# A tuned attention-plus-MLP kernel: order of the first loads and a new order of steps

## The chip, the core and the metric

The kernel runs on one core of one Trainium2 chip. TensorE (PE) multiplies, VectorE (DVE), ScalarE (ACT) and GpSimd (POOL) work elementwise, and the queue of SyncE (SP) issues nearly all DMAs. The metric is the device time of the program in microseconds; lower is better. All times below are microseconds unless marked otherwise.

## The reference

The input x is [2048, 512] in bf16. It is layer-normalised, goes through two branches, and both results are added to x:

```python
xn = _layernorm(x, axis=-1)
return x + _A_ref(xn, A_wqkv, A_w_phi, A_wo) + _B_ref(xn, B_w1, B_b1, B_w2)
```

Branch A is linear attention with 32 heads of 16. Queries and keys are multiplied per head by w_phi [16, 16]; the feature map is softmax(p) beside softmax(-p):

```python
phi_k = jnp.concatenate([_softmax(pk, axis=-1), _softmax(-pk, axis=-1)], axis=-1)
kv = jnp.einsum("bhsf,bhsd->bhfd", phi_k, v)
num = jnp.einsum("bhqf,bhfd->bhqd", phi_q, kv)
```

The numerator is divided by phi_q times the sum of phi_k, and the heads are multiplied by wo [512, 512]. Branch B is h = xn w1 + b1 with 1792 columns, h tanh(softplus(h)), and w2 back to 512.

## The kernel before

The 2048 rows are 16 tiles of 128, in four groups of four. x, all weights, the transposed normalised rows xnT and the activations acts of branch B stay on chip. w_phi is folded into the weights: the keys' and the queries' parts of wqkv are turned, multiplied by Wbd (w_phi laid out as a block diagonal) and copied back, so that a projection of xn gives the logits of the feature map directly.

The order of all work is written out by hand in the string STEPS (line 24). Each step is a name and its arguments; a number behind @ is the PSUM bank (there are six, plus one double bank called kv) and a letter a or v says whether ScalarE or VectorE makes the copy. Lines 620 to 643 map names to functions and run the steps. Each engine executes its instructions in the order in which the steps issue them, and a wait blocks what stands behind it on that engine. A step that takes a bank waits until the copy out of its last content is done.

The names that matter here:

- LS i, RS i, AZ i (lines 547 to 557): mean and variance of tile i of the first group on VectorE, its 1/sqrt on POOL (two instructions), its centring on VectorE. TP i turns the centred tile by TensorE, TC i copies it into xnT.
- TW kt and TK kt (566 to 578): TensorE turns the natural half (kt 0 and 1) of the keys' weights wkp, ScalarE copies it into wT. The other half of wT comes turned by a DMA (line 482). WB makes Wbd from w_phi (wsrc). F0 kt (line 146) folds, FD kt copies the fold back into wkp. LP (line 196) makes the first two key logits, eight matmuls; with "i" the two tiles alternate, so each FD releases one pair.
- PB and CB turn the bias b1 and copy it. KM makes a mask from constants.
- LN g, AP g k, DX g: statistics, centring plus DMA transposes, and loads of the later groups. WT, F, FC: the queries' weights, turned by DMA and folded later. DW loads w2 and wo.
- V t and VC t: value projection and its copy. L s i and LC s i: logits of tile i in stage s (0 to 3 keys, 4 to 7 queries) and their copy; WL the same in the kv bank. H u and M u: one of 56 blocks of the hidden layer and its activation.
- E s p, X s k, S s k: extremes and subtraction (five VectorE instructions), exponential on ScalarE, sums on VectorE. R and N: reciprocal and normalisation of the keys. A g k: accumulation of kv. KV masks it. W s k: weights of the queries and their DMA transposes. Q, G, C: the queries' product, its copies, the division with a DMA transpose.
- O t, P t, Y t: second layer, output projection, residual and store. OH, PH, YH do the last tile in two parts.

Ahead of the steps stand the first loads (lines 476 to 492) and WARM + SHORT dummy matmuls of 512 and 128 columns on constants (line 517). The loads of x, wqkv and w1 go through SP's queue, those of the bias and of w_phi through ScalarE's. The order on SP is x tile 0, x tile 1, the natural half of the keys' weights, the turned half, then the rest.

Of the kernel before, what the change touches and what calls it, by code (L numbers as in the profile page):

```python
# [21 lines left out]
STEPS = """
TW 0 @0; TW 1 @1; LS 0; LS 1; RS 0; PB @2; KM; AZ 0; TK 0 a; RS 1; DX 2; WB; TP 0 @3; F0 0 @4; AZ 1;
TP 1 @5; TK 1 a; FD 0 a; TC 0 v; F0 1 @0; F0 2 @1; FD 1 a; F0 3 @3; FD 2 a; TC 1 v; LS 2; RS 2; FD 3
a; LS 3; CB; LP i @4,5; V 1 @0; AZ 2; LC 0 0 v; RS 3; AZ 3; TP 2 @1; V 0 @3; LC 0 1 v; TC 2 a; TP 3
@2; L 0 2 @4; VC 0 a; TC 3 v; H 0 @1; L 0 3 @5; LC 0 2 a; LC 0 3 a; LN 1; H 1 @3; H 2 @2; H 3 @4; M
0; M 1; H 4 @5; VC 1 a; M 2; H 5 @1; H 6 @3; H 7 @0; M 3; M 4; H 8 @2; M 5; M 6; H 9 @4; H 10 @5; E
0 0; M 7; H 11 @1; AP 1 0; L 1 0 @3; WL 1; AP 1 1; M 8; V 6 @0; E 0 1; X 0 0; LN 2; VC 6 v; X 0 1;  # L30
DX 3; LN 3; LC 1 0 a; L 1 3 @2; LC 1 3 a; AP 2 0; AP 2 1; WL 2; M 9; H 12 @0; H 13 @3; M 10; H 14
@2; H 15 @4; H 16 @5; M 11; M 12; M 13; M 14; M 15; M 16; H 17 @1; LC 1 1 a; S 0 1; H 18 @0; M 17;
AP 3 0; AP 3 1; M 18; S 0 0; H 19 @3; H 20 @2; H 21 @4; H 22 @5; M 19; M 20; H 23 @1; H 24 @0; M 21;
M 22; M 23; M 24; LC 1 2 v; E 1 0; E 1 1; H 25 @3; H 26 @2; H 27 @4; H 28 @5; H 29 @1; V 2 @0; VC 2
v; DW 3; M 25; M 26; M 27; M 28; M 29; R 0 0 a; L 2 1 @3; L 2 0 @2; WT; L 2 2 @4; LC 2 0 a; R 0 1 a;
LC 2 1 v; F 0 @5; F 1 @1; N 0 0; FC 0 a; FC 1 a; F 2 @0; V 3 @3; LC 2 2 a; X 1 1; L 3 0 @2; VC 3 a;
FC 2 v; N 0 1; F 3 @5; FC 3 a; LC 3 0 v; L 2 3 @0; X 1 0; V 4 @1; L 3 3 @4; DW 2; LC 2 3 v; L 3 1
@2; VC 4 a; LC 3 3 a; V 8 @0; V 5 @3; VC 5 a; V 9 @5; A 0 0; VC 9 a; LC 3 1 a; E 2 0; E 2 1; L 4 0
@1; S 1 0; L 3 2 @4; VC 8 a; S 1 1; X 2 0; H 30 @3; S 2 0; LC 4 0 a; L 4 3 @5; LC 4 3 a; LC 3 2 a; L
4 2 @2; LC 4 2 a; L 4 1 @0; V 7 @1; VC 7 v; A 0 1; R 1 0 a; LC 4 1 a; E 3 0; R 1 1 a; H 31 @5; H 32  # L40
@4; H 33 @2; E 3 1; H 34 @0; H 35 @1; M 30; M 31; N 1 0; M 32; M 33; M 34; H 36 @3; M 35; H 37 @5; H
38 @4; M 36; M 37; M 38; H 39 @2; N 1 1; M 39; H 40 @0; H 41 @1; H 42 @3; M 40; M 41; H 43 @5; A 1
0; A 1 1; M 42; V 13 @4; L 6 1 @2; E 4 0; E 4 1; V 10 @0; V 15 @1; VC 10 v; M 43; L 6 0 @3; O 0 @5;
X 3 0; V 12 @0; X 2 1; X 3 1; LC 6 0 v; LC 6 1 v; X 4 0; S 3 0; VC 13 a; R 3 0 a; VC 15 a; S 2 1; R
2 1 a; V 11 @3; O 1 @2; VC 11 a; L 5 0 @4; VC 12 a; L 6 3 @1; R 2 0 a; LC 6 3 a; S 4 0; LC 5 0 a; L
6 2 @3; LC 6 2 a; S 3 1; L 5 1 @0; LC 5 1 a; L 5 2 @1; L 5 3 @4; R 3 1 a; LC 5 2 a; LC 5 3 a; V 14
@3; VC 14 a; H 44 @0; N 2 0; N 3 0; N 3 1; H 45 @1; X 4 1; M 44; N 2 1; H 46 @4; H 47 @3; M 45; M
46; A 2 0; W 4 0 v; M 47; A 2 1; A 3 0; S 4 1; A 3 1; H 48 @0; M 48; H 49 @1; M 49; H 50 @4; L 7 0
@3; H 51 @0; M 50; M 51; H 52 @1; H 53 @4; KV; W 4 1 v; E 5 0; E 5 1; M 52; M 53; H 54 @0; M 54; Q 0
0; G 0 0; E 6 0; H 55 @1; O 2 @4; M 55; X 5 0; Q 0 1; LC 7 0 a; S 5 0; O 3 @0; G 0 1; Q 1 0; L 7 3  # L50
@1; C 0 a; G 1 0; LC 7 3 a; L 7 1 @3; LC 7 1 a; W 5 0 v; Q 1 1; G 1 1; X 5 1; E 6 1; O 4 @1; C 1 a;
L 7 2 @3; LC 7 2 a; P 0; P 1; Q 2 0; G 2 0; S 5 1; Y 0; O 5 @3; W 5 1 a; Q 2 1; P 2; X 6 0; P 3; O 6
@5; G 2 1; E 7 0; C 2 a; Q 3 0; Y 1; Y 2; O 7 @2; S 6 0; Y 3; W 6 0 v; G 3 0; Q 3 1; E 7 1; P 4; O 8
@4; G 3 1; C 3 a; O 9 @0; Q 4 0; Y 4; X 6 1; S 6 1; P 5; W 6 1 v; O 10 @1; Y 5; G 4 0; X 7 0; S 7 0;
Q 4 1; G 4 1; C 4 a; W 7 0 v; X 7 1; O 11 @3; Q 5 0; P 6; P 7; Y 6; G 5 0; Q 5 1; S 7 1; O 12 @5; G
5 1; Q 6 0; C 5 a; W 7 1 a; Y 7; P 8; P 9; G 6 0; Q 6 1; G 6 1; O 13 @2; Q 7 0; Y 8; P 10; Y 9; G 7
0; P 11; Q 7 1; O 14 @4; G 7 1; C 6 v; P 12; P 13; Y 10; Y 11; C 7 a; Y 12; OH 0 @0; PH 0; P 14; OH
1 @1; Y 13; YH 0; Y 14; PH 1; YH 1
"""


# [612 lines left out]
```

## Time and profile before

| what | value |
| --- | --- |
| time, median of 3 runs | 173.48 us (173.38 to 173.89) |
| profiled execution, time | 173.81 us |
| profiled execution, span | 172.1 us |
| PE busy | 166.6 us (97%), 1031 matmuls |
| DVE busy | 144.6 us (84%) |
| ACT busy | 119.0 us (69%) |
| POOL busy | 9.3 us (5%) |
| matmuls of the hidden layer (line 222) | 49.8 us, 224 of 379 ns |
| matmuls of the second layer (line 456) | 50.3 us, 231 |
| natural half of the keys' weights, 256 KB | 3.7 us from issue to landing |
| x tiles 0 and 1, 128 KB each | 2.1 us from issue to landing |
| w_phi, 16 KB | 4.1 us from issue to landing |

The profile shows one execution from its first to its last instruction. A line of a timeline has the start, the length, the engine, the line of the kernel, the operation and what it writes from what it reads; in brackets stands the idle time before it and what ended that. Matmuls are pipelined: a 512-wide one is listed with 379 ns, but the next starts 0.216 us later. Some matmul records are missing in the trace, so counts can be a few below those of the program.

### The profile page before, as it was taken

How to read it: one execution, taken by the hardware profiler on the slowest of the kernel's cores; microseconds unless marked ns; L12 is line 12 of the kernel's file. 1: busy time of each engine (PE TensorE's matmuls, PEld its weight loads, DVE VectorE, ACT ScalarE, POOL GpSimd, SP SyncE). 2: the span in 40 equal slices, each digit the busy share in tenths (PEclk: the TensorE clock that was granted, in tenths of full speed). 3: DMA queues.
4: the chain of work that ended last, by engine and by line, in shares of the span. 5: the costliest groups of instructions: out<-in, count | busy, mean ns of one | idle time of the engine just before them, and what ended most of it. 6: DMA issues, size and time to landing. Idle time of an engine off the chain costs nothing.

```text
span 172.1 us, 2711 instructions
## 1 busy us (share of the span) xinstructions
PE 166.6 (97%) x1031; PEld 82.7 (48%) x1047; DVE 144.6 (84%) x223; ACT 119.0 (69%) x192; POOL 9.3 (5%) x26
## 2 busy tenths in 40 slices
...
GB/s 122 292 369 261 49 197 0 121 140 259 352 47 0 0 4 0 0 0 4 0 0 0 71 91 86 0 55 132 92 148 128 123 94 152 141 141 212 144 101 61
DMA packets 44185, 18.02 MB, mean 105 GB/s; under 512 B 35980, under 2 KB 44172, under 8 KB 44172
## 3 DMA queue, kind: packets, MB, share of 16 engines
...
q8 instruction: 8, 0.13, 0.3%
q14 instruction: 5, 0.04, 0.1%
...
## 4 chain that ended last, share of the span: by engine, by line
PE 92%; DMA 2%; ACT 2%; DVE 1%; issue 1%; SPq 0%; DVEq 0%
PE ph L222 28%; PE po L456 28%; PE pl L188 14%; PE po L463 8%; PE pv L188 7%; PE pnd L411 2%; PE pkv L380 2%; DMA wkp<-in_A_wqkv_dram 2%; ACT wkp L159 1%; PE pwide L188 1%; PE pfold L150 1%; ACT wT L575 0%; SPq L477 0%; DVE m L257 0%; DVE p_sb L246 0%
## 5 line engine op out<-in xcount | busy, mean ns | idle before, releaser
L456 PE MATMUL po<-w_sb,acts 128*128 128x512 bf16 (+2 forms) x231 | 50.3, 366 | 0.3
L222 PE MATMUL ph<-xnT,w_sb 128*128 128x512 bf16 x224 | 49.8, 379 | 0.0
L233 ACT ACTIVATE acts<-ph,b1f 128x512 bf16<-128x512 f32 x56 | 36.3, 698 | 5.5 <-PE ph L222 5.3
L299 DVE TENSOR_REDUCE s<-e 128x128 f32<-128x2048 bf16 x16 | 36.1, 2279 | 1.7 <-ACT e L282 1.7
L222 PEld LDWEIGHTS <-w_sb 128*128 128x128 bf16 x224 | 21.7, 98 | 25.7
L456 PEld LDWEIGHTS <-acts 128*128 128x128 bf16 x238 | 22.3, 98 | 24.1
L282 ACT ACTIVATE e<-e 128x2048 bf16<-128x2048 bf16 x16 | 30.2, 1911 | 0.0
L188 PEld LDWEIGHTS <-xnT 128*128 128x128 bf16 x184 | 17.6, 98 | 20.1
L426 ACT COPY ds<-pnd 128x32 f32<-128x32 f32 x16 | 3.0, 185 | 22.0 <-PE pnd L411 22.0
L470 DVE TENSOR_TENSOR x_sb<-po,x_sb 128x512 bf16<-128x512 f32 (+2 forms) x17 | 11.1, 657 | 8.3 <-PE po L463 8.3
L188 PE MATMUL pv<-wv,xnT 128*128 128x512 bf16 x62 | 15.7, 379 | 0.1
L246 ACT CAST p_sb<-pl 128x512 bf16<-128x512 f32 x23 | 12.9, 592 | 4.0 <-PE pl L188 4.0
L463 PE MATMUL po<-wqk,xnT 128*128 128x512 bf16 (+2 forms) x66 | 15.3, 366 | 0.1
L188 PE MATMUL pl<-wqk,xnT 128*128 128x512 bf16 x62 | 15.0, 379 | 0.1
L164 DVE BATCH_NORM_STATS2 stats<-x_sb 128x6 f32<-128x512 bf16 x16 | 10.1, 678 | 3.6 <-DMA x_sb<-in_A_x_dram 3.6
L257 DVE TENSOR_TENSOR m<-m 128x512 bf16<-128x512 bf16 (+1 forms) x32 | 11.5, 359 | 1.1
L188 PE MATMUL pl<-wkp,xnT 128*128 128x512 bf16 x46 | 11.7, 379 | 0.1
L257 DVE TENSOR_TENSOR m<-p_sb 128x1024 bf16<-128x1024 bf16 x16 | 10.9, 684 | 0.1
L266 DVE TENSOR_TENSOR e<-p_sb,m 128x2048 bf16<-128x2048 bf16 x8 | 9.8, 1226 | 1.0 <-PE pkv L380 0.5
L266 DVE TENSOR_TENSOR e<-m,p_sb 128x2048 bf16<-128x2048 bf16 x8 | 9.8, 1226 | 0.3
L333 DVE TENSOR_TENSOR e<-e,r 128x2048 bf16<-128x2048 bf16 x8 | 9.4, 1218 | 0.4 <-ACT r L308 0.4
...
## 6 DMA issues: line engine op xcount, KB each, us to landing
...
```

The lines of the kernel that those rows point to most:

```text
L164: nc.vector.bn_stats(stats[:, i, :], xs[:, i, :])
L188: nc.tensor.matmul(pp, lhsT=xnT[:, t, kt, :], rhs=w[:, kt, :], start=(kt == 0), stop=(kt == KT - 1),)
L222: nc.tensor.matmul(ph_of[u][:], lhsT=w1_sb[:, kt, f * P : (f + 1) * P], rhs=xnT[:, g * TPG : (g + 1) * TPG, kt, :], start=(kt == 0), stop= ...
L233: nc.scalar.activation(acts[:, f, g * 512 : (g + 1) * 512], ph_of.pop(u)[:], ACT.Mish, bias=b1f[:, f : f + 1])
L246: copy(p_of[s][:, i, :], pl_of.pop((s, i)))
L257: nc.vector.tensor_tensor(out=m[:], in0=src[:, :, 0:half], in1=src[:, :, half : 2 * half], op=op)
L266: nc.vector.tensor_tensor(out=e_of[s][:].rearrange("p t j l c -> p (t j) l c")[:, :, pl, :].rearrange("p t (c e o) -> p t c e o", e=8, o=2 ...
L282: nc.scalar.activation(v, v, ACT.Exp)
L299: nc.vector.reduce_sum(t[:], pair(s, k).rearrange("p t j l (c e) -> p (t j l c) e", e=16), axis=AX.X)
L456: nc.tensor.matmul(po_of[t, c.stop][:, c], lhsT=acts[:, f, t * P : (t + 1) * P], rhs=w2_sb[:, f, c], start=(f == 0), stop=False,)
L463: nc.tensor.matmul(po_of[t, c.stop][:, c], lhsT=oT_of[t // 2][:, t % 2 * 4 + j, :], rhs=wo_sb[:, j, c], start=False, stop=(j == 3),)
L470: nc.vector.tensor_tensor(out=y, in0=po_of.pop((t, c.stop))[:, c], in1=y, op=ALU.add)
```

## The change

Three things change. On SP the natural half of the keys' weights is issued between x tile 0 and x tile 1, and on ScalarE's queue w_phi is issued ahead of the bias. The dummy matmuls are 8 of 512 columns and 4 of 128, in place of 9 and 3. And STEPS is written anew: all 437 steps remain, but their order, their banks and for fourteen of them the copying engine differ. In the head, LS 1 stands ahead of AZ 0 and WB, KM comes after the first tiles, and PB and CB come later. The diff, with the new order cut to its head and the parts that the prediction speaks of:

```diff
-WARM, SHORT = 9, 3
+WARM, SHORT = 8, 4
 STEPS = """
-TW 0 @0; TW 1 @1; LS 0; LS 1; RS 0; PB @2; KM; AZ 0; TK 0 a; RS 1; DX 2; WB; TP 0 @3; F0 0 @4; AZ 1;
-TP 1 @5; TK 1 a; FD 0 a; TC 0 v; F0 1 @0; F0 2 @1; FD 1 a; F0 3 @3; FD 2 a; TC 1 v; LS 2; RS 2; FD 3
-a; LS 3; CB; LP i @4,5; V 1 @0; AZ 2; LC 0 0 v; RS 3; AZ 3; TP 2 @1; V 0 @3; LC 0 1 v; TC 2 a; TP 3
...
+LS 0; RS 0; LS 1; TW 0 @0; TK 0 a; AZ 0; TW 1 @1; WB; TK 1 a; TP 0 @2; F0 0 @3; FD 0 a; RS 1; AZ 1;
+TC 0 v; F0 1 @4; TP 1 @5; F0 2 @0; FD 1 a; TC 1 v; LS 2; RS 2; PB @1; CB; FD 2 a; LS 3; F0 3 @2; FD
+3 a; LP i @3,5; V 1 @4; AZ 2; TP 2 @0; RS 3; TC 2 a; V 0 @1; AZ 3; TP 3 @2; LC 0 0 a; LC 0 1 a; KM;
+VC 1 a; L 0 2 @0; LC 0 2 a; TC 3 v; H 0 @3; VC 0 a; M 0; H 1 @2; L 0 3 @5; LN 1; LC 0 3 a; H 2 @4; H
+3 @0; H 4 @1; DX 2; H 5 @3; M 1; M 2; M 3; M 4; H 6 @5; M 5; M 6; H 7 @2; H 8 @4; H 9 @0; E 0 0; AP
...
+42; N 1 0; H 43 @1; A 1 0; A 1 1; E 4 0; V 12 @0; E 4 1; VC 12 v; M 43; X 3 1; L 6 0 @2; LC 6 0 v; L
+6 1 @5; X 2 1; S 2 1; L 6 2 @4; LC 6 2 a; X 3 0; S 3 0; V 14 @3; L 5 0 @1; V 15 @0; O 0 @2; LC 5 0
...
+P 11; Q 7 1; G 7 1; Y 9; O 14 @5; OH 0 @4; Y 10; P 12; P 13; C 7 a; P 14; PH 0; OH 1 @0; PH 1; Y 11;
+Y 12; Y 13; Y 14; YH 0; YH 1
 """
...
-    for t in range(2):
-        nc.sync.dma_start(x_sb[:, t, :], x_v[:, t, :])
+    nc.sync.dma_start(x_sb[:, 0, :], x_v[:, 0, :])
 
 
     wT_of = {0: lnp.tile([P, 4, 512], BF16, name="wT", tag="xn")}
     nc.sync.dma_start(wkp[:, 0:2, :], wqkv_v[:, 0:2, D : 2 * D])
+    nc.sync.dma_start(x_sb[:, 1, :], x_v[:, 1, :])
     nc.sync.dma_start_transpose(
         out=wT_of[0][:, :, 2 * P : 4 * P], in_=A_wqkv[2 * P : 4 * P, D : 2 * D]
     )
-    nc.scalar.dma_start(b1b[:], b1_v[:, :])
     with nc.allow_non_contiguous_dma(reason="tiny w_phi load"):
         nc.scalar.dma_start(wsrc[:], wphi_v)
+    nc.scalar.dma_start(b1b[:], b1_v[:, :])
```

More of the change, by code (lines that the diff above doesn't have):

```diff
@@ L14 @@
 AX = mybir.AxisListType
-WARM, SHORT = 9, 3
+WARM, SHORT = 8, 4
 STEPS = """
-TW 0 @0; TW 1 @1; LS 0; LS 1; RS 0; PB @2; KM; AZ 0; TK 0 a; RS 1; DX 2; WB; TP 0 @3; F0 0 @4; AZ 1;
-TP 1 @5; TK 1 a; FD 0 a; TC 0 v; F0 1 @0; F0 2 @1; FD 1 a; F0 3 @3; FD 2 a; TC 1 v; LS 2; RS 2; FD 3
-a; LS 3; CB; LP i @4,5; V 1 @0; AZ 2; LC 0 0 v; RS 3; AZ 3; TP 2 @1; V 0 @3; LC 0 1 v; TC 2 a; TP 3
-@2; L 0 2 @4; VC 0 a; TC 3 v; H 0 @1; L 0 3 @5; LC 0 2 a; LC 0 3 a; LN 1; H 1 @3; H 2 @2; H 3 @4; M
-0; M 1; H 4 @5; VC 1 a; M 2; H 5 @1; H 6 @3; H 7 @0; M 3; M 4; H 8 @2; M 5; M 6; H 9 @4; H 10 @5; E
@@ L30 @@
[L30 to L58, printed above, removed]
+LS 0; RS 0; LS 1; TW 0 @0; TK 0 a; AZ 0; TW 1 @1; WB; TK 1 a; TP 0 @2; F0 0 @3; FD 0 a; RS 1; AZ 1;
+TC 0 v; F0 1 @4; TP 1 @5; F0 2 @0; FD 1 a; TC 1 v; LS 2; RS 2; PB @1; CB; FD 2 a; LS 3; F0 3 @2; FD
@@ new lines @@
+3 a; LP i @3,5; V 1 @4; AZ 2; TP 2 @0; RS 3; TC 2 a; V 0 @1; AZ 3; TP 3 @2; LC 0 0 a; LC 0 1 a; KM;
+VC 1 a; L 0 2 @0; LC 0 2 a; TC 3 v; H 0 @3; VC 0 a; M 0; H 1 @2; L 0 3 @5; LN 1; LC 0 3 a; H 2 @4; H
+3 @0; H 4 @1; DX 2; H 5 @3; M 1; M 2; M 3; M 4; H 6 @5; M 5; M 6; H 7 @2; H 8 @4; H 9 @0; E 0 0; AP
+1 0; AP 1 1; DX 3; M 7; E 0 1; LN 2; M 8; M 9; H 10 @1; H 11 @3; H 12 @5; X 0 1; X 0 0; M 10; M 11;
+L 1 0 @2; V 6 @4; VC 6 v; L 1 3 @0; WL 1; LC 1 0 a; LC 1 3 v; WL 2; LN 3; H 13 @4; AP 2 0; S 0 1; AP
@@ new lines @@
+2 1; AP 3 0; M 12; AP 3 1; H 14 @0; M 13; LC 1 2 a; H 15 @1; H 16 @3; M 14; M 15; M 16; LC 1 1 a; H
+17 @2; H 18 @5; H 19 @4; M 17; H 20 @0; S 0 0; H 21 @1; M 18; H 22 @3; WT; M 19; H 23 @2; M 20; M
+21; M 22; H 24 @5; H 25 @4; H 26 @0; H 27 @1; M 23; M 24; M 25; M 26; M 27; H 28 @3; M 28; E 1 0; E
+1 1; H 29 @2; M 29; L 2 0 @5; LC 2 0 v; L 2 3 @4; LC 2 3 v; R 0 0 a; L 2 2 @0; LC 2 2 a; F 0 @1; FC
+0 v; L 2 1 @3; R 0 1 a; N 0 0; N 0 1; F 1 @2; V 7 @5; F 2 @4; VC 7 v; LC 2 1 a; FC 2 v; F 3 @0; X 1
@@ new lines @@
+0; L 3 0 @1; FC 3 a; A 0 0; FC 1 a; V 3 @3; DW 2; VC 3 a; E 2 0; LC 3 0 a; L 3 2 @5; LC 3 2 a; V 2
+@0; X 1 1; L 4 3 @4; V 8 @2; VC 8 a; V 9 @3; VC 9 a; E 2 1; VC 2 v; L 3 3 @1; L 3 1 @5; LC 3 3 a; V
+11 @2; X 2 0; L 4 0 @3; LC 4 0 a; LC 3 1 a; LC 4 3 a; V 4 @0; S 1 1; S 1 0; L 4 2 @1; LC 4 2 a; R 1
+1 a; VC 4 a; A 0 1; H 30 @3; VC 11 a; R 1 0 a; N 1 1; L 4 1 @5; V 5 @4; H 31 @1; H 32 @0; LC 4 1 v;
+H 33 @2; VC 5 a; M 30; S 2 0; M 31; M 32; E 3 0; M 33; H 34 @5; DW 3; E 3 1; H 35 @4; H 36 @3; H 37
@@ new lines @@
+@1; M 34; M 35; M 36; M 37; H 38 @0; H 39 @2; M 38; H 40 @5; H 41 @4; M 39; M 40; M 41; H 42 @3; M
+42; N 1 0; H 43 @1; A 1 0; A 1 1; E 4 0; V 12 @0; E 4 1; VC 12 v; M 43; X 3 1; L 6 0 @2; LC 6 0 v; L
+6 1 @5; X 2 1; S 2 1; L 6 2 @4; LC 6 2 a; X 3 0; S 3 0; V 14 @3; L 5 0 @1; V 15 @0; O 0 @2; LC 5 0
+a; VC 14 a; X 4 0; L 6 3 @4; S 3 1; L 5 2 @1; VC 15 a; LC 5 2 a; R 2 0 a; L 5 1 @3; LC 5 1 a; S 4 0;
+R 3 1 a; V 10 @0; VC 10 a; R 2 1 a; O 1 @1; N 3 1; R 3 0 a; LC 6 1 a; V 13 @3; VC 13 a; L 5 3 @0; LC
@@ new lines @@
+6 3 a; LC 5 3 a; X 4 1; N 2 0; H 44 @5; H 45 @3; N 2 1; M 44; N 3 0; A 2 0; M 45; H 46 @4; M 46; A 2
+1; S 4 1; A 3 0; A 3 1; W 4 0 v; W 4 1 v; KV; L 7 3 @0; H 47 @5; H 48 @3; M 47; M 48; H 49 @4; H 50
+@5; H 51 @3; M 49; M 50; E 5 0; M 51; H 52 @4; M 52; H 53 @5; M 53; E 5 1; Q 0 0; E 6 0; H 54 @3; G
+0 0; M 54; H 55 @4; M 55; Q 0 1; O 2 @5; G 0 1; C 0 a; X 5 0; Q 1 0; G 1 0; S 5 0; W 5 0 v; L 7 0
+@3; LC 7 0 a; O 3 @4; LC 7 3 a; Q 1 1; X 5 1; L 7 2 @3; O 4 @0; G 1 1; S 5 1; C 1 a; LC 7 2 a; P 0;
```

5 lines of the change are left out of this document (added).

## The prediction

> **What bounds the kernel now.** I read the profile in this order: busy shares, a table of stages, the chain of waits, the timeline of the head by engine, and the transfers. The stages first; their columns are the stretch, its length, then busy time of TensorE (PE), its weight loads, VectorE (DVE), ScalarE (ACT) and GpSimd (POOL), the granted clock and the DMA share.
>
> ```profile
> 0.00:4.39 4.39, 3.56 (x12) 1.41 (x12) 1.38 (x3) 1.28 (x1) 2.07 (x14) 1.00 0.47 126
> 4.39:5.47 1.08, 0.01 (x1) 0.00 (x1) 0.78 (x4) 0.00 (x0) 1.00 (x3) 1.00 1.22 173
> 5.47:9.52 4.05, 3.92 (x41) 2.67 (x43) 3.28 (x10) 3.12 (x6) 1.20 (x4) 1.00 1.10 344
> 9.52:169.44 159.92, 159.12 (x980) 78.59 (x993) 138.83 (x207) 114.56 (x185) 5.06 (x8) 1.00 0.44 98
> 169.44:172.10 2.66, 0.00 (x0) 0.00 (x0) 0.29 (x1) 0.00 (x0) 0.00 (x0) 1.00 0.20 62
> ```
>
> From 9.52, where V 1 starts, to 169.44 TensorE has no hole: it is the bound, its work is the same in both kernels, and an order can only lose there. What can be won lies ahead of 9.52; 2.66 us of tail follow the last matmul. So the sum is: when does V 1 start, does the new body open a hole, and what does the tail do.
>
> The chain of waits (start, length, what) shows what sets 9.52:
>
> ```profile
> 1.72 3.71 DMA wkp<-in_A_wqkv_dram
> ...
> 5.91 0.25 ACT wT L575
> ...
> 6.98 2.06 ACT wkp L159 x4
> 9.04 0.04 issue
> 9.09 0.59 PE pl L203 x2
> 9.68 0.86 PE pv L188 x4
> ```
>
> The natural half of the keys' weights lands at 5.43; TW, TK, F0 and four copies FD follow on ScalarE, and the last pair of LP waits for FD 3. Tile 1 is not on this chain. The timeline of VectorE shows how early it is:
>
> ```profile
> 2.98 0.69 DVE L164 BATCH_NORM_STATS2 stats<-x_sb 128x6 f32<-128x512 bf16 x1 [2.98 <-DMA x_sb<-in_A_x_dram]
> 3.71 0.18 DVE L166 BATCH_NORM_AGGREGATE mv<-stats 128x2 f32<-128x6 f32 x1
> 3.81 0.66 DVE L164 BATCH_NORM_STATS2 stats<-x_sb 128x6 f32<-128x512 bf16 x1
> 4.50 0.18 DVE L166 BATCH_NORM_AGGREGATE mv<-stats 128x2 f32<-128x6 f32 x1
> 4.60 0.19 DVE L521 TENSOR_TENSOR KVmask<-block 128x64 f32<-128x64 bf16 x1
> 4.91 0.41 DVE L175 TENSOR_SCALAR xn<-x_sb,mv,rstd 128x512 bf16<-128x512 bf16 x1
> 5.63 0.43 DVE L526 TENSOR_TENSOR Wbd<-block,wsrc 128x512 bf16<-128x512 bf16 x1 [0.31 <-DMA wsrc<-in_A_w_phi_dram]
> 5.98 0.41 DVE L175 TENSOR_SCALAR xn<-x_sb,mv,rstd 128x512 bf16<-128x512 bf16 x1
> ```
>
> LS 1 at 3.81 waited for nothing (its tile landed at 3.32 by the landing records). WB waited for w_phi, which landed at 5.61.
>
> **The change, part by part.** *Warm-ups.* One 512-wide dummy becomes a 128-wide one. They end at 4.39; at full clock one is 0.22 us, the other 0.06, so they end 0.16 earlier, inside the 1.08 us in which TensorE waits for wkp. Cost 0; without that wait it would be a gain of 0.16.
>
> *Transfers.* SP issues x0 at 0.79, x1 at 1.25, wkp at 1.72. Now wkp goes at 1.25 and x1 at 1.72. wkp: if it keeps its 3.71 us it lands at 4.96. By bytes: SP's queue had moved 0.27 MB by 3.00 (both tiles) and 0.13 MB more by 3.90, which is what x0 and wkp hold together, and wkp's landing came 0.43 after its last piece at 5.0, so 4.35 is the other end. I take 4.4. x1: two bounds. Its own issue-to-landing time (2.07 us) put at 1.72 gives 3.79; the place in the bytes that wkp's end had gives 5.43. Between 3.00 and 3.50 the DMA share fell to 0.33 while w_phi's 512 pieces of 32 B ran beside the load; w_phi is issued at 1.48, its pieces start about 1.25 later and last to 5.0. It is now issued at 0.78, so this dip moves onto x0 and wkp, and x1 comes behind both. I take 4.8, above the middle (4.61), because the bytes ahead of it on its queue are a harder row than the time of a tile that had only 128 KB before it. w_phi itself lands near 5.61 - 0.70 = 4.9; the bias follows it and isn't needed before PB (about 7.7).
>
> The Trainium skill's page "DMA: Bandwidth & Descriptors", section on queues, rings and completion order, says that each DMA engine takes turns between the queues that have work for it, a packet at a time. By that rule w_phi's pieces cost the SP queue the same total wherever they stand, and x1 would land at the late end. The dip to 0.33 at 3.00 to 3.50 doesn't contradict it, but shows idle engines, which taking turns alone does not give.
>
> *Head order.* VectorE executes in order, and LS 1 now stands ahead of AZ 0 and WB with a wait for x1. Behind it queue AZ 0 (TP 0 waits for it), WB (F0 0), AZ 1 (TP 1) and TC 0, TC 1 (LP). With x1 at L: stats start L+0.02; from there to that tile's AZ it is 2.98 to 4.91 = 1.93 in the rows above (statistics 0.73, two POOL steps with their hand-overs 1.20); AZ 1 0.41; TP 1 0.05 + 0.39; TC 1 0.03 + 0.42; LP 0.09 later; LP is now held by the tile and not by the last fold, so its 8 matmuls run through: 8 x 0.216 = 1.73. Sum: V 1 starts at L + 5.07. ScalarE's side: AZ 0 at L+0.85, WB at L+1.2, F0 0 at L+1.7, FD 0 at L+2.1, four copies of 0.5, so FD 3 ends at L+4.2, before LP's last pair at L+4.65: the old wait goes, tile 1 is late next. wkp at 4.4 (TK 1 done at 6.0) is no longer on the path. With L = 4.8, V 1 starts at 9.87 instead of 9.52: **+0.35**. Bounds: L = 3.79 gives 8.86 (-0.66), L = 5.43 gives 10.50 (+0.98). Break-even is L = 4.45.
>
> *Body.* I counted, step by step, the TensorE work that stands ahead of each step in both orders, and the DVE and ACT work ahead of what it waits for, with durations of the rows (512-wide matmul 0.216, copy 0.60 on DVE at pitch and 0.48 on ACT, E 2.96, sum 2.19, norm 1.14, Exp 1.81, Mish 0.57). In total three LC, two W and smaller ones change engine: DVE 143.5 to 141.0, ACT 110.3 to 112.4; seven table loads in both. The tight places: E 0 0 waits for LC 0 3, and L 0 3 stands one H (0.86) later, so DVE starts E 0 0 at 16.4 instead of 15.57; it has 1.03 idle before VC 6 at 26.56, which takes that up. A 1 1 stands 0.86 later, and E 4 0's last step waits for it (75.25 in the trace, 0.20 after A 1 1 ends); from there E 4 1 and VC 12 take 4.11 + 0.69, and V 15, which takes VC 12's bank, stands 6 x 0.864 = 5.18 after A 1 1: 0.18 spare. KV ends near 102.2 (S 4 1 waits for X 4 1, now behind two moved copies), Q 0 0 stands at 105.2. W 7 1 hands to SP at 153.4, its transposes land 157.3, Q 7 0 stands at 158.1. None stops: +0. On SP's queue, DX 2 still precedes the first AP and waits for nothing, DX 3 still follows AP 1 1, WT follows AP 3 1 (issue about 38, landing 7.1 later, F 0 at 46.7), DW 2 and DW 3 have 20 us and more to O 0 and P 0. KM (0.19) falls into the 0.51 that DVE idles before TC 3.
>
> *Tail.* Y 11 to Y 14 are now together behind C 7; Y 14 and YH 0 change places. VectorE has idles of 2 us there, YH 1 still follows PH 1: 0, between -0.1 and +0.15 for four stores close together on the queue ahead of the last.
>
> Sum: 0 + 0.35 + 0 + 0. The profiled execution took 173.81 (span 172.1, 1.7 around it), so its like is 174.16; the median of the three runs shown, 173.48, is 0.33 below, and I forecast against it: 173.48 + 0.35 = **173.83**.
>
> **The rivals.** *x1 lands soon after its issue.* 3.79 to 3.9, as two bare tiles did in 2.1 us; the free DMA share at 3.00 to 3.50 speaks for it, 256 KB ahead of it against. V 1 at 8.86: 173.48 - 0.66 = 172.8, faster. *x1 lands where wkp did.* Between 3.00 and 3.90 w_phi's queue moved 151 pieces and SP's 141, about one for one; if that costs the same wherever w_phi stands, only the bytes count. The dip speaks against it. V 1 at 10.50: 174.46, slower; it decides from L = 4.97 on (+0.52). *V 15 waits for VC 12.* If DVE reaches E 4 0's last step late, say with the 0.9 of E 0 0 not made up, TensorE stops for 0.7: with the head 174.5, slower; against it speaks that by the count DVE stands there 1.2 early (75.0, A 1 1 ends at 76.2). *The clock falls.* After TW, TensorE waits from 4.9 to about 6.1 for AZ 0 and is thin up to LP; at the slow pace of the first dummies (0.427 per 512-wide matmul, from 0.82 to 3.34) as long a stretch, 2.5 us, would cost +1.25: 175.1. Before, a wait of 1.08 left the pitch at 0.056 per 128-wide one, which speaks against it. The Trainium skill, "TensorE: Matmul & The Clock Gate", Part 1, puts the fall at an idle window of about 3.4 us; no run here shows such a gap, and by that rule it doesn't happen.
>
> **How the numbers follow.** A measurement of this kernel can tell about 0.3% (0.52 us). x1 in the middle, body dense: 0.43, 173.83. x1 early: 0.20, faster. x1 late: 0.20, slower. V 15 or another hole in the body: 0.14, slower. Clock: 0.03, slower. So faster 0.20, same 0.43, slower 0.37. The likeliest case's own range is L 4.4 to 4.95: 173.4 to 174.0. Half the early case lies below 172.85, and the body's worst and the clock lie above 174.7; these are the ends.
>
> **What would show it.** LS 1 waiting for x_sb until about 4.8 and AZ 0 behind it at 5.65 instead of 4.91; TW 0 at 4.4; LP without a break, V 1 at 9.87; no wait named before any matmul after that; V 15 close behind VC 12. Wrong if LS 1 starts below 4 or above 5, or TensorE shows holes after 10 us.

## The result: slower by 0.35 percent, and where the profile after shows it

| | before | after |
| --- | --- | --- |
| median | 173.72 us (173.38 to 174.10, 8 runs) | 174.40 us (174.20 to 174.66, 8 runs) |
| profiled execution, time and span | 173.81 us, 172.1 | 174.66 us, 172.9 |
| x tile 1 landed | 3.32 | 5.16 |
| natural half of the keys' weights landed | 5.43 | 4.17 |
| w_phi landed | 5.61 | 3.16 |
| values' weights wv landed | 8.96 | 10.31 (15 of 16 engines by 8.76) |
| V 1 starts | 9.52 | 10.35 |

The ratio of the times is 1.0035, with an interval of 1.0019 to 1.0050 (the quotient of the two medians is 1.0039). The forecast was 173.83, +0.35 us; measured is +0.68 between the medians and +0.85 between the two profiled executions. The time lies in the range. The ratio is just past the 0.3% that I had set as the bound of no change, but its interval reaches below that bound; that the kernel is slower at all is clear.

The table of stages of after, with cuts at the end of the dummies, at WB (6.30), at V 1 and at the last matmul. Columns as there.

```profile
0.00:4.83 4.83, 4.00 (x14) 1.80 (x15) 0.88 (x2) 1.28 (x1) 2.50 (x14) 1.00 0.59 139
4.83:6.30 1.47, 0.85 (x8) 0.58 (x6) 1.09 (x3) 1.01 (x2) 0.18 (x2) 1.00 1.07 245
6.30:10.35 4.05, 3.62 (x34) 2.29 (x34) 3.22 (x11) 2.21 (x5) 1.61 (x5) 1.00 1.04 350
10.35:170.27 159.92, 159.92 (x995) 78.50 (x993) 136.23 (x204) 116.75 (x191) 5.13 (x8) 1.00 0.44 96
170.27:172.90 2.63, 0.00 (x0) 0.00 (x0) 0.29 (x1) 0.00 (x0) 0.00 (x0) 1.00 0.30 94
```

From V 1 to the last matmul it is 159.92 us, to the hundredth what it was before: 437 steps in another order, and no hole. The tail is 2.63 against 2.66. All of the difference stands ahead of V 1, which starts 0.83 later. The chain of waits of after (start, length, what) says by what:

```profile
1.71 3.44 DMA x_sb<-in_A_x_dram
...
5.18 0.70 DVE stats L164
...
6.55 0.62 POOL rstd L171
7.17 0.03 issue
7.20 0.42 DVE xn L175
...
7.67 0.40 PE ptr L562 x4
...
8.73 1.73 PE pl L203 x8
```

The keys' weights, their turn and their folds have left the chain; tile 1 with its statistics has taken their place. The timeline of VectorE in after shows the queue behind LS 1:

```profile
5.18 0.69 DVE L164 BATCH_NORM_STATS2 stats<-x_sb 128x6 f32<-128x512 bf16 x1 [1.27 <-DMA x_sb<-in_A_x_dram]
5.91 0.18 DVE L166 BATCH_NORM_AGGREGATE mv<-stats 128x2 f32<-128x6 f32 x1
6.00 0.38 DVE L175 TENSOR_SCALAR xn<-x_sb,mv,rstd 128x512 bf16<-128x512 bf16 x1
6.30 0.42 DVE L526 TENSOR_TENSOR Wbd<-block,wsrc 128x512 bf16<-128x512 bf16 x1
7.20 0.41 DVE L175 TENSOR_SCALAR xn<-x_sb,mv,rstd 128x512 bf16<-128x512 bf16 x1 [0.48 <-POOL rstd L171]
```

VectorE idles 1.27 ahead of LS 1, for the tile; AZ 0 (6.00) and WB (6.30) are held by it although tile 0 and w_phi are long there; AZ 1 at 7.20 waits for POOL's 1/sqrt. On TensorE, after, the same as waits:

```profile
6.44 0.40 PE L562 MATMUL ptr<-ident,xn 128*128 128x128 bf16 x4 [0.77 <-DVE xn L175]
...
7.67 0.40 PE L562 MATMUL ptr<-ident,xn 128*128 128x128 bf16 x4 [0.29 <-DVE xn L175]
...
8.56 1.89 PE L203 MATMUL pl<-wkp,xnT 128*128 128x512 bf16 x8
10.35 1.02 PE L188 MATMUL pv<-wv,xnT 128*128 128x512 bf16 x4
```

LP runs its eight matmuls without a break and V 1 follows at once. It could hardly have started sooner: one of the sixteen engines that carry wv delivered its part at 10.31. (The landing records count sixteen parts for each of these loads; I read a part as one engine's share.)

### The profile page after: what moved, and what is told of

It reads as the page before. It is cut to its first block, busy times and chain, and to the rows that moved or that the text cites. A ratio compares the mean times of both kernels' runs of the same rounds, so it can differ in the third digit from the quotient of the medians.

```text
span 172.9 us, 2728 instructions
## 1 busy us (share of the span) xinstructions
PE 168.4 (97%) x1047; PEld 83.2 (48%) x1047; DVE 141.7 (82%) x219; ACT 121.3 (70%) x198; POOL 9.4 (5%) x26
## 4 chain that ended last, share of the span: by engine, by line
PE 94%; DMA 2%; DVE 1%; POOL 1%; SPq 0%; issue 0%
PE po L456 28%; PE ph L222 28%; PE pl L188 14%; PE pv L188 8%; PE po L463 8%; PE pnd L411 2%; PE pkv L380 2%; DMA x_sb<-in_A_x_dram 2%; PE pwide L188 1%; PE pl L203 1%; PE pfold L150 1%; PE ptr L562 0%; DVE stats L164 0%; POOL rstd L171 0%; DVE xn L175 0%
## 5 line engine op out<-in xcount | busy, mean ns | idle before, releaser
L456 PE MATMUL po<-w_sb,acts 128*128 128x512 bf16 (+2 forms) x238 | 51.0, 366 | 0.0
L233 ACT ACTIVATE acts<-ph,b1f 128x512 bf16<-128x512 f32 x56 | 36.8, 701 | 5.3 <-PE ph L222 5.1
L188 PEld LDWEIGHTS <-xnT 128*128 128x128 bf16 x184 | 17.3, 98 | 19.2 <-issue 0.2
L188 PE MATMUL pv<-wv,xnT 128*128 128x512 bf16 x64 | 16.3, 379 | 0.0
L188 PE MATMUL pl<-wqk,xnT 128*128 128x512 bf16 x64 | 15.8, 379 | 0.0
L246 ACT CAST p_sb<-pl 128x512 bf16<-128x512 f32 x25 | 14.0, 586 | 2.3 <-PE pl L188 2.2
L463 PEld LDWEIGHTS <-xnT 128*128 128x128 bf16 x68 | 6.3, 98 | 6.4
```

The source lines that it names most:

```text
L188: nc.tensor.matmul(pp, lhsT=xnT[:, t, kt, :], rhs=w[:, kt, :], start=(kt == 0), stop=(kt == KT - 1),)
L233: nc.scalar.activation(acts[:, f, g * 512 : (g + 1) * 512], ph_of.pop(u)[:], ACT.Mish, bias=b1f[:, f : f + 1])
L246: copy(p_of[s][:, i, :], pl_of.pop((s, i)))
L456: nc.tensor.matmul(po_of[t, c.stop][:, c], lhsT=acts[:, f, t * P : (t + 1) * P], rhs=w2_sb[:, f, c], start=(f == 0), stop=False,)
L463: nc.tensor.matmul(po_of[t, c.stop][:, c], lhsT=oT_of[t // 2][:, t % 2 * 4 + j, :], rhs=wo_sb[:, j, c], start=False, stop=(j == 3),)
```

## The experiments

Two questions. Why did tile 1 land at 5.16 and not at 4.8? And is tile 1 the only thing that holds V 1? My theory at first was that tile 1, behind the keys' weights, sets the end alone, so that bringing it earlier gives the time back. The rivals were the turned half behind it, the place of LS 1 in VectorE's order, the clock, the landing of wv, and the new order of steps itself.

Before the single runs, the reading that ties them together. In the profiled execution of every kernel I take the start of V 1 from TensorE's timeline, and that execution's own time:

| kernel | V 1 starts | its time | time less V 1 | what V 1's start ended on |
| --- | --- | --- | --- | --- |
| new_steps_old_loads | 9.50 | 173.82 | 164.32 | keys' weights, then the folds' order on TensorE |
| before | 9.52 | 173.81 | 164.29 | keys' weights and folds |
| w_phi_behind_keys | 9.57 | 173.87 | 164.30 | wv |
| before_turned_half_later | 9.61 | 173.89 | 164.28 | keys' weights and folds |
| turned_half_later | 9.62 | 173.92 | 164.30 | tile 1 |
| before_w_phi_first | 9.97 | 174.28 | 164.31 | wv |
| x1_first | 10.02 | 174.36 | 164.34 | wv |
| turned_half_later_again | 10.05 | 174.37 | 164.32 | wv |
| warm_nine | 10.09 | 174.41 | 164.32 | tile 1 |
| old_steps_new_loads | 10.27 | 174.61 | 164.34 | tile 1, then the folds |
| bias_first | 10.29 | 174.61 | 164.32 | tile 1 |
| after | 10.35 | 174.66 | 164.31 | tile 1 |
| before_w_phi_first_turned_later | 10.61 | 174.94 | 164.33 | wv |
| ls1_behind_wb | 12.12 | 176.41 | 164.29 | LS 1's place on VectorE, then the clock |

In these fourteen executions of thirteen kernels, with two orders of steps (in ls1_behind_wb one step of the head is moved as well), the time less V 1's start lies between 164.28 and 164.34. The body and the tail are a constant here; an execution is as good as its V 1. So each experiment is read by what V 1 waited for. One profile shows one execution, though: where the times of a kernel spread over more than a microsecond, as those of x1_first do (174.31 to 175.69, profiled at 174.36), what held the slower ones is not seen. In new_steps_old_loads and x1_first the profile puts TensorE's wait ahead of TW down to POOL; the keys' weights had landed 0.04 to 0.05 before TW began (5.04 and 5.09, 5.26 and 5.30), as in before, so I read these waits as theirs.

**Tile 1 issued first again.** After, with x tile 1 back ahead of the keys' weights; w_phi stays ahead of the bias.

```diff
 nc.sync.dma_start(x_sb[:, 0, :], x_v[:, 0, :])
+nc.sync.dma_start(x_sb[:, 1, :], x_v[:, 1, :])
 nc.sync.dma_start(wkp[:, 0:2, :], wqkv_v[:, 0:2, D : 2 * D])
-nc.sync.dma_start(x_sb[:, 1, :], x_v[:, 1, :])
```

> The changed kernel, with x tile 1 issued ahead of the natural half again (w_phi still ahead of the bias, new steps kept). If the loss comes from x tile 1 landing late and nothing else, LS 1 starts near 3.8 and the old chain through the natural half decides: V 1 about 4.1 after that half has landed, so 9.1 to 9.5 and a time at or below that of the kernel before (0.997 to 1.000 of it). If the new order of the body or the fewer warm-ups cost it, the time stays at 1.0035 of the kernel before. How early the natural half lands tells more: by the bytes and the earlier w_phi at 4.4 to 4.9; if the turned half that follows on the queue holds back the completions of the load ahead of it, at 5.1 or later.

Measured: 174.89 us (174.31 to 175.69), ratio 1.0076, interval 1.0049 to 1.0102: no better than after. Tile 1 landed at 3.66, so the first theory would have the time back. The keys' weights now landed at 5.26 (15 of 16 parts from 5.09 on, behind pieces of the turned half that end together at 5.03 to 5.07), and LP began at 7.99, 0.57 earlier than in after. But the chain of waits of x1_first goes another way:

```profile
4.16 5.81 DMA wv<-in_A_wqkv_dram
9.97 0.04 issue
10.02 1.02 PE pv L188 x4
```

V 1 waited for wv. By the landing records, 13 engines had delivered it by 8.45 and three at 9.81 to 9.97; x tiles 2 and 3, issued ahead of it, show the same split (13 by 7.01, three at 8.34 to 8.52). Tile 1 is not the only thing that holds V 1; my first theory falls.

**LS 1 behind WB.** After, with the statistics of tile 1 taken out of the way of AZ 0 and WB.

```diff
-LS 0; RS 0; LS 1; TW 0 @0; TK 0 a; AZ 0; TW 1 @1; WB; TK 1 a; TP 0 @2; F0 0 @3; FD 0 a; RS 1; AZ 1;
+LS 0; RS 0; TW 0 @0; TK 0 a; AZ 0; TW 1 @1; WB; LS 1; TK 1 a; TP 0 @2; F0 0 @3; FD 0 a; RS 1; AZ 1;
```

> The changed kernel, with LS 1 moved behind WB, so that AZ 0 and WB no longer wait behind it on VectorE. If tile 1's own path (land, statistics, root, centring, turn, copy) sets V 1, nothing moves: AZ 0 at about 4.9, F0 0 at about 6, but V 1 at 10.2 to 10.4 and a time within 0.1% of the changed kernel. If the loss was the queue behind LS 1, the folds come 0.7 to 1 earlier and V 1 with them, at 9.4 to 9.6, 0.4% to 0.5% below the changed kernel.

Measured: 176.64 us (176.41 to 176.72), ratio 1.0164, interval 1.0148 to 1.0181: 2.2 us slower than after. TP 0 did start earlier, at 5.43 instead of 6.44, and the folds behind it at 5.76. But LS 1 now waited its turn on VectorE: tile 1 had landed at 4.92, and its statistics began at 5.62, behind AZ 0 and WB. VectorE's timeline there:

```profile
5.29 0.42 DVE L526 TENSOR_TENSOR Wbd<-block,wsrc 128x512 bf16<-128x512 bf16 x1
5.62 0.69 DVE L164 BATCH_NORM_STATS2 stats<-x_sb 128x6 f32<-128x512 bf16 x1
```

With that TensorE ran dry before tile 1 was ready. The table of stretches of ls1_behind_wb (TensorE's busy time is the first figure behind the length, the granted clock the last but two):

```profile
5.50:6.50 1.00, 1.00 (x12) 0.64 (x12) 0.97 (x3) 0.87 (x3) 0.00 (x0) 1.00 0.88 219
6.50:7.50 1.00, 0.00 (x1) 0.00 (x0) 0.03 (x1) 0.76 (x2) 0.80 (x2) 1.00 0.82 266
7.50:8.50 1.00, 0.49 (x5) 0.49 (x6) 0.74 (x2) 0.00 (x0) 0.01 (x1) 0.69 1.13 352
8.50:9.50 1.00, 1.00 (x11) 0.78 (x9) 0.84 (x2) 0.42 (x1) 0.00 (x0) 0.50 1.00 357
9.50:10.50 1.00, 1.00 (x5) 0.45 (x4) 0.97 (x4) 0.75 (x2) 0.43 (x2) 0.50 1.01 377
10.50:11.50 1.00, 1.00 (x4) 0.33 (x4) 0.65 (x3) 0.00 (x0) 0.92 (x3) 0.61 1.08 381
```

and TensorE's timeline there:

```profile
8.01 0.61 PE L562 MATMUL ptr<-ident,xn 128*128 128x128 bf16 x4 [1.51 <-DVE xn L175]
...
9.50 2.78 PE L203 MATMUL pl<-wkp,xnT 128*128 128x512 bf16 x7
12.12 1.03 PE L188 MATMUL pv<-wv,xnT 128*128 128x512 bf16 x4
```

A gap of 1.51 us, and the clock record of the trace shows half speed from 7.88 to 11.29; LP takes 2.62 instead of 1.79 from its first matmul to V 1. This is the fourth rival of the prediction, the clock. In after, LS 1 holds AZ 0 back, and TensorE's gaps are 0.77 and 0.29, without a fall. The clock record moves in steps of 3.41 us, so I cut both kernels into such stretches. ls1_behind_wb, the stretch that ended in the fall and the one at half speed:

```profile
4.46:7.88 3.42, 1.78 (x24) 1.24 (x21) 1.87 (x6) 2.15 (x4) 1.27 (x3) 1.00 0.99 255
7.88:11.29 3.41, 3.28 (x18) 1.96 (x19) 2.84 (x9) 1.17 (x2) 1.14 (x4) 0.50 1.05 369
```

and after, its thinnest stretch at full speed, which it had from 5.84 on:

```profile
5.84:9.25 3.41, 2.52 (x29) 1.83 (x30) 2.71 (x9) 2.52 (x6) 0.90 (x2) 1.00 1.04 328
```

A third kernel narrows it. In before_w_phi_first_turned_later (below) TensorE waited 1.38 us for the keys' weights, and its first stretch at full speed was thinner still than that of after:

```profile
3.88:7.29 3.41, 2.02 (x24) 1.30 (x23) 2.49 (x9) 0.88 (x2) 1.61 (x4) 1.00 1.06 220
```

The clock fell behind the stretch with 1.78 us of matmuls in 3.42, and did not behind those with 2.02 and 2.52 in 3.41. Whether the sum of the matmuls decides or the length of the gap (1.51 against 1.38 and 0.77), these three cannot tell. The Trainium skill, "TensorE: Matmul & The Clock Gate", Part 1, lets the clock fall after an idle window of about 3.4 us. The length of the fall, 3.41, agrees with its window; the condition does not, since no such stretch was idle here. The measurement decides.

**The turned half later.** After, with the DMA transpose behind x tiles 2 and 3 on SP's queue.

```diff
 nc.sync.dma_start(x_sb[:, 1, :], x_v[:, 1, :])
-nc.sync.dma_start_transpose(
-    out=wT_of[0][:, :, 2 * P : 4 * P], in_=A_wqkv[2 * P : 4 * P, D : 2 * D]
-)
...
 nc.sync.dma_start(x_sb[:, 2:4, :], x_v[:, 2:4, :])
+nc.sync.dma_start_transpose(
+    out=wT_of[0][:, :, 2 * P : 4 * P], in_=A_wqkv[2 * P : 4 * P, D : 2 * D]
+)
```

The reason to try it stands in after's landing records: ten of tile 1's sixteen parts were complete at 3.93 to 4.47 and six at 5.10 to 5.16, though all its data had moved by 4.10. The turned half moves in pieces of 256 bytes, most of which take 0.02 us; about twenty take longer and end together, at 5.06 to 5.12. The six late parts of tile 1 come with that common end.

> The changed kernel, with the transfer that loads the turned half of the keys' weights issued behind x tiles 2 and 3 instead of ahead of them. If the landing of x tile 1 is set by the bytes ahead of it, it stays near 5.1 and so do V 1 (10.3) and the time. If the turned half holds back the completions of the load just ahead of it, x tile 1 lands at 4.2 to 4.5, V 1 starts at 9.4 to 9.7 and the time falls by 0.35% to 0.5%, to the kernel before or just below. The turned half itself lands about 0.7 later (7.0), and F0 2 may wait for it a little.

Measured: 174.39 us (173.89 to 175.04), ratio 1.0036, interval 1.0021 to 1.0051. In the profile tile 1 lands at 4.47, V 1 starts at 9.62 and the execution takes 173.92, all as the theory wants; the median is after's. The chain of waits of turned_half_later:

```profile
1.70 2.77 DMA x_sb<-in_A_x_dram
4.47 0.02 issue
4.49 0.70 DVE stats L164
```

The load that now stands ahead of the turned half is held in its place: 13 of the 16 parts of x tiles 2 and 3 come at 5.90 to 6.09, with the turned half's common end at 5.91 to 5.96. Nothing waits for them here.

**The same once more**, to see what its other executions wait for.

> The kernel after with the turned half of the keys' weights issued behind x tiles 2 and 3, once more. Its profiled execution had tile 1 landed at 4.47 and V 1 started at 9.62, 0.7 earlier than after, and took 173.92; yet its median was 174.39 and its times lay between 173.89 and 175.04. Theory 1: what spreads the times is the landing of the values' weights, on single DMA engines 1 us and more behind the others in some executions. Then a profiled execution that takes 174.3 or more shows V 1 waiting for wv beyond 10.0, and one near 173.9 shows wv landed by 9.0. Theory 2: the time is lost behind V 1, in the body. Then a profiled execution of 174.3 or more shows V 1 near 9.6 with a span from V 1 to the last matmul above 159.92. Median by both: 174.2 to 174.6.

Measured: 174.34 us (173.84 to 175.67), ratio 1.0041, interval 1.0019 to 1.0063, and this time the profiled execution is one of 174.37. Its chain and, below it, its TensorE timeline:

```profile
4.09 5.92 DMA wv<-in_A_wqkv_dram
10.01 0.04 issue
10.05 1.02 PE pv L188 x4
```

```profile
7.80 1.89 PE L203 MATMUL pl<-wkp,xnT 128*128 128x512 bf16 x7
10.05 1.02 PE L188 MATMUL pv<-wv,xnT 128*128 128x512 bf16 x4 [0.36 <-DMA wv<-in_A_wqkv_dram]
```

Tile 1 landed at 4.39 and LP began at 7.80, both a little earlier than in the first profile. But wv, complete at 8.66 there, took until 10.01 here (nine engines by 8.22, the last five between 9.00 and 10.01). V 1 starts 0.43 later, and the execution takes 0.45 longer. One kernel, two executions, one difference: theory 1 of this run holds for these two; the longest executions, up to 175.67, were not profiled. Two things are shown: the turned half behind tile 1 costs it 0.45 to 0.77 us (4.47 and 4.39 without it; 4.92 to 5.16 in the five kernels that have it right behind), and taking that away doesn't bring the median back. In the execution of 174.37 it is wv that was next.

**The turned half later, in before.**

```diff
 nc.sync.dma_start(wkp[:, 0:2, :], wqkv_v[:, 0:2, D : 2 * D])
-nc.sync.dma_start_transpose(
-    out=wT_of[0][:, :, 2 * P : 4 * P], in_=A_wqkv[2 * P : 4 * P, D : 2 * D]
-)
...
 nc.sync.dma_start(x_sb[:, 2:4, :], x_v[:, 2:4, :])
+nc.sync.dma_start_transpose(
+    out=wT_of[0][:, :, 2 * P : 4 * P], in_=A_wqkv[2 * P : 4 * P, D : 2 * D]
+)
```

> The kernel before, with the turned half of the keys' weights issued behind x tiles 2 and 3. If that transfer holds back the completions of the load ahead of it, here the natural half, this lands at 4.9 to 5.1 instead of 5.43 and V 1 starts at 9.0 to 9.3 instead of 9.52: a time of 0.997 to 0.999 of the kernel before, if F0 2 (7.03) doesn't come to wait for the turned half, which lands at about 7.1. If the bytes and w_phi set it, the natural half stays at 5.43 and the time is the same or a little longer.

Measured: 173.83 us (173.50 to 174.17), ratio 1.0009, interval 0.9999 to 1.0018: no change. The keys' weights land at 5.51 instead of 5.43. In before all their parts come at 5.23 to 5.43, right with the turned half's common end at 5.22 to 5.26. Here they come one by one from 4.26 to 5.51, beside w_phi's parts from 3.45 to 5.70: most parts are free earlier, the last is not. That w_phi's small pieces hold the last ones is a guess that two runs below don't settle: the keys' weights land at 4.73 with w_phi behind them on SP's queue, but at 5.93 with w_phi early and the turned half late.

**w_phi first, in before.** This is the change's second edit alone.

```diff
-nc.scalar.dma_start(b1b[:], b1_v[:, :])
 with nc.allow_non_contiguous_dma(reason="tiny w_phi load"):
     nc.scalar.dma_start(wsrc[:], wphi_v)
+nc.scalar.dma_start(b1b[:], b1_v[:, :])
```

> The kernel before, with w_phi issued ahead of the bias and nothing else. Two theories. If w_phi's small pieces only slow the load that runs beside them, the natural half of the keys' weights lands at 5.05 to 5.25 instead of 5.43, V 1 starts at 9.1 to 9.35, and the time is 0.997 to 0.9985 of the kernel before. If w_phi first makes later loads late (the value weights wv landed at 10.31, 9.97 and 9.74 in three of the four kernels with it, at 8.96 in the kernel before), V 1 waits for wv at 9.6 to 10.3 and the time is 1.001 to 1.005 of it.

Measured: 174.69 us (173.76 to 175.76), ratio 1.0049, interval 1.0028 to 1.0071. This one edit costs about as much as the whole change (the intervals overlap). w_phi lands at 3.45, the keys' weights at 5.31 (15 of 16 parts between 5.10 and 5.31: the turned half's common end again, now on them), LP begins 0.11 earlier than in before. And the waits of TensorE in before_w_phi_first are:

```profile
PE ptw L569 <- DMA wkp<-in_A_wqkv_dram: 0.6, 1, 0.6
PE pv L188 <- DMA wv<-in_A_wqkv_dram: 0.4, 1, 0.4
```

Three engines bring wv at 9.86 to 9.93, the other thirteen by 8.70.

**Both of these in before.** w_phi ahead of the bias, and the turned half behind x tiles 2 and 3; the diff is the last two together.

> The kernel before, with w_phi ahead of the bias and the turned half behind x tiles 2 and 3. Neither w_phi nor the turned half is then beside or right behind the natural half, which should land at 4.3 to 4.6; ScalarE's chain gives V 1 at 8.6 to 9.0, and the time is 0.995 to 0.998 of the kernel before if wv has landed by then (8.7 to 9.0). If w_phi first makes wv late, V 1 waits until 9.6 or later and the time is 1.000 to 1.005, with a wide spread between runs.

Measured: 174.85 us (173.65 to 176.5), ratio 1.0048, interval 1.0029 to 1.0066. In the profiled execution the keys' weights come at 5.93 and wv at 10.57 (three engines from 10.03, the rest by 9.18); V 1 starts at 10.61. The expectation was 4.3 to 4.6 for the keys' weights, and this is a miss that no theory here explains: nine parts came by 4.54 and seven from 5.00 to 5.93, though w_phi's pieces were over at 2.95 and the turned half came behind x tiles 2 and 3. What spreads these parts is open. The 176.5 is an execution with a mean granted clock of 0.99.

**The bias first, in after.** This takes the second edit back and leaves the others.

```diff
+nc.scalar.dma_start(b1b[:], b1_v[:, :])
 with nc.allow_non_contiguous_dma(reason="tiny w_phi load"):
     nc.scalar.dma_start(wsrc[:], wphi_v)
-nc.scalar.dma_start(b1b[:], b1_v[:, :])
```

> The changed kernel, with the bias ahead of w_phi again. x tile 1 sits beside w_phi's pieces then and lands at 5.1 to 5.6, so V 1 starts at 10.3 to 10.8 and the time is 1.003 to 1.006 of the kernel before, whatever wv does. What tells the theories apart is wv: 8.7 to 9.0 with no engine more than 0.4 behind the others if w_phi first is what makes it late, 9.7 or later in an engine or more if it is the order on SP's queue.

Measured: 176.22 us (174.53 to 177.12), ratio 1.0122, interval 1.0077 to 1.0166. Two of the six executions, with a granted clock of 1.0, took 174.53 and 174.61; the four others show 0.989 to 0.990 and took 176.10 to 177.12. The profiled one is of the first sort: tile 1 at 5.16 and V 1 at 10.29, as in after. So w_phi's place does not decide when tile 1 lands (5.16 both times), and the order on SP's queue alone is enough for the late V 1. wv came at 10.12, with 15 parts by 9.05, so w_phi ahead of the bias is not needed to make it late either. With the bias first the granted clock is lower in four executions of six, in after in none of eight. That the four are a fall like that of ls1_behind_wb fits their times and clock, but none of them was profiled.

**Nine dummies again, in after.**

```diff
-WARM, SHORT = 8, 4
+WARM, SHORT = 9, 3
```

> The changed kernel, with 9 long and 3 short warm-up matmuls again. The warm-ups ended at 4.83 and TensorE waits for the first tile from 5.7 to 6.4 in the changed kernel, so nothing should move: 0.999 to 1.001 of the changed kernel. If the fewer warm-ups cost something through the clock, the time falls by 0.2% or more.

Measured: 174.55 us (174.41 to 174.60), ratio 1.0044, interval 1.0030 to 1.0059, which overlaps after's. No cost of the number of dummies shows.

**The new steps with the old loads.** After, with the five load lines of before. The dummies stay 8 and 4.

```diff
-nc.sync.dma_start(x_sb[:, 0, :], x_v[:, 0, :])
+for t in range(2):
+    nc.sync.dma_start(x_sb[:, t, :], x_v[:, t, :])
 nc.sync.dma_start(wkp[:, 0:2, :], wqkv_v[:, 0:2, D : 2 * D])
-nc.sync.dma_start(x_sb[:, 1, :], x_v[:, 1, :])
...
+nc.scalar.dma_start(b1b[:], b1_v[:, :])
 with nc.allow_non_contiguous_dma(reason="tiny w_phi load"):
     nc.scalar.dma_start(wsrc[:], wphi_v)
-nc.scalar.dma_start(b1b[:], b1_v[:, :])
```

> The changed kernel (new steps, 8 and 4 warm-ups) with the loads in the order of the kernel before, on both queues. If the whole loss is in the order of the loads, LS 1 runs from 3.8, V 1 starts at 9.4 to 9.7 and the time is 0.999 to 1.001 of the kernel before. If the new steps cost something of themselves, it stays at 1.002 or more.

Measured: 174.01 us (173.78 to 175.80), ratio 1.0027, interval 1.0003 to 1.0051. Its profiled execution is that of before within 0.02: V 1 at 9.50, 173.82. Its median is 0.17 us above that of before on the same chip. Ten of its twelve executions took 173.78 to 174.35, the other two 175.40 and 175.80 at full clock; these were not profiled, and what held them is open.

**The old steps with the new loads.** The counterpart: before with the load lines of after, and 9 and 3 dummies.

> The kernel before (old steps, 9 and 3 warm-ups) with the loads in the changed order, on both queues. LS 1 stands ahead of AZ 0 and WB in the old steps too, so by the theory of the loads x tile 1 lands at 4.9 to 5.2, V 1 starts at 10.1 to 10.4 and the time is 1.0035 to 1.005 of the kernel before, like the changed kernel. If it is the steps, the time is at most 1.001.

Measured: 174.70 us (174.54 to 174.78), ratio 1.0055, interval 1.0039 to 1.0071. Its chain:

```profile
1.71 3.21 DMA x_sb<-in_A_x_dram
...
7.09 0.42 DVE xn L175
...
8.22 1.57 ACT wkp L159 x3
9.79 0.04 issue
9.84 0.59 PE pl L203 x2
```

Tile 1 holds AZ 1, TP 1 and, through the order on TensorE, the later folds, whose copies then hold LP's last pair. From its landing (4.92) to V 1 it is 5.35 here, against 5.19 in after. In ratios the new steps alone cost 0.27% (the interval begins at 0.03%), the new loads alone 0.55%, and both together 0.35%; the intervals are too wide to say whether they add up. In the profiled executions it is 0.01, 0.80 and 0.85 us. So the new loads bring the loss; that the new steps lose anything by themselves is not shown.

**w_phi behind the keys' weights.** Before, with w_phi taken off ScalarE's queue and issued on SP's behind the natural half. I hoped for a kernel better than both.

```diff
 nc.sync.dma_start(wkp[:, 0:2, :], wqkv_v[:, 0:2, D : 2 * D])
+with nc.allow_non_contiguous_dma(reason="tiny w_phi load"):
+    nc.sync.dma_start(wsrc[:], wphi_v)
...
-with nc.allow_non_contiguous_dma(reason="tiny w_phi load"):
-    nc.scalar.dma_start(wsrc[:], wphi_v)
```

> The kernel before, with w_phi taken off ScalarE's queue and issued on SP's behind the natural half of the keys' weights, ahead of the turned half. Its pieces can then not run beside the natural half. By the theory that they slow it, the natural half lands at 4.2 to 4.8 instead of 5.43; w_phi lands at 5.1 to 5.6 and lets F0 0 start at 5.8 to 6.2 (6.54 before), V 1 at 8.9 to 9.2, a time of 0.996 to 0.998 of the kernel before. If engines fall behind for another reason than w_phi's place on its queue, wv lands at 9.7 or later and V 1 waits for it, 1.002 or more.

Measured: 174.05 us (173.70 to 175.06), ratio 1.0027, interval 1.0008 to 1.0046. The keys' weights land at 4.73, 0.70 earlier than in before, and TensorE's timeline shows what becomes of it:

```profile
7.12 1.96 PE L203 MATMUL pl<-wkp,xnT 128*128 128x512 bf16 x7
9.57 1.04 PE L188 MATMUL pv<-wv,xnT 128*128 128x512 bf16 x4 [0.49 <-DMA wv<-in_A_wqkv_dram]
```

LP begins 0.59 earlier than in before (7.71), and V 1 waits 0.49 for wv, whose last three engines come at 9.26 to 9.52. This is the clearest reading of the second limit: even the fastest head is stopped there. Before, with wv at 8.96 and V 1 at 9.52, has only about 0.5 to gain. None of the kernels is faster than before.

## Why the prediction came out right in its direction and short in its size

The forecast missed 174.40 by 0.57. Of this, 0.24 is the base: I forecast from the 173.48 of three runs, and the median of eight is 173.72. The other 0.33 is the change itself, +0.68 where I had +0.35. That the time lies in the range doesn't make the likeliest case right. No change had 0.43, the late tile 0.20, and what came is the late tile, which the range was wide enough to hold. By my own sign, LS 1 above 5, the prediction was wrong at this point: LS 1 started at 5.18.

*Which stage decides* held: the body is 159.92 in both, and V 1's start sets the time in all fourteen profiled executions. The terms of the body, 0, and of the tail, 0, are right; V 15 did not wait for VC 12, so that rival is out.

*What is late next* held for after: LS 1 waits for x_sb, AZ 0 and WB stand behind it, LP runs without a break, and the wait for FD 3 is gone.

*The landing of the keys' weights* was taken as 4.4 and came at 4.17, below the lower end of 4.35. w_phi was put near 4.9 and came at 3.16: its pieces ran from 2.18 to 2.83, where in before they lasted from 2.76 to 5.02. Neither is on after's chain of waits.

*The landing of tile 1* is the term that was mis-sized. I took 4.8 and it was 5.16, inside my bounds of 3.79 to 5.43 but 0.36 late. I weighed only the bytes ahead of tile 1 and w_phi's pieces beside it. What decided stands behind it on its queue, the turned half: with that moved, tile 1 lands at 4.47 and 4.39, close to the break-even of 4.45. The rule of taking turns, which I named from the Trainium skill ("DMA: Bandwidth & Descriptors", queues, rings and completion order), would have put it at the late end; 4.39 with all of w_phi's pieces still ahead says that they cost tile 1 little. The same section of the Trainium skill ties a completion to the earlier writes of its engine; here a load that was issued later held the completion back, which that by itself doesn't give.

*From tile 1 to V 1* I had 5.07, and it was 5.19: AZ 1 came 2.04 after the landing where I had 1.95, and LP took 1.79 where I had 1.73. The sum of both errors, 0.36 and 0.12, is what V 1 is later than forecast (10.35 against 9.87). So the result lies at the rival "x1 lands where wkp did", 174.46, which I had decided from 4.97 on, though its cause, w_phi's bytes, is not the one found. That 174.40 and 174.46 agree so closely is luck in part: the rival's V 1 was 10.50 where 10.35 was measured, and the low base made up for it.

*What I left out* is wv. No term and no rival of the prediction names it, and it landed 0.04 ahead of V 1 in after. Had tile 1 come early, V 1 could not have started before 10.31 in that execution: the rival of 172.8, with V 1 at 8.86, was not to be had, and its 0.20 was too much. With wv as in before, at 8.96, it would have cost that rival its best 0.1 only; with 9.3 to 10.6, where most of the runs with new loads had it, nothing is left of its gain or little.

*The dummies* cost nothing, as said, but not by ending 0.16 earlier: they ended at 4.83 instead of 4.39. The clock record gives full speed from 5.84 in after and from 3.47 in before. In warm_nine it is 5.75 with before's number of dummies, so their number is not what differs.

*The clock* did not fall in after. I had priced it by a slow stretch of 2.5 us, at +1.25; where it fell, with LS 1 moved, a gap of 1.51 was enough (one of 1.38 in another kernel was not), it lasted 3.41, and V 1 came 1.77 later than in after. It was nearer than the 0.03 that I gave it, and the idle window that I named as the condition is not needed.

What stays open: why one to five engines fall about a microsecond behind the others between 6 and 10 us. The last part of wv came at 9.30 or later in ten of the eleven profiled executions whose first loads are issued in another order than before's, and at 8.58 to 8.96 in the three in which x tile 1, the keys' weights, the bias and w_phi go as in before. In some of the ten x tiles 2 and 3 show as many late parts (three in x1_first), in others none (after). No run separates a cause.
